# An attention kernel: one of four slices of VectorE's exponentials made in place by an accumulating DMA, with three buffers of clamped scores

## The chip, the cores and the metric

The kernel runs on one core of a Trainium2 chip. A core has five engines that run side by side, each through its own list of instructions in order: PE (TensorE, matrix products), ACT (ScalarE, functions such as exp), DVE (VectorE, elementwise work), POOL (GpSimd, elementwise work and DMA) and SP (SyncE, here only for starting DMAs). They wait for each other through semaphores. Times are microseconds (us) of the device for one execution; lower is better.

## The reference

One input x (2048 tokens, 640 features) goes through two attention branches of 32 heads with 20 features each. Branch A is full softmax attention; branch B lets each token see itself and the seven tokens 2, 4, ... 14 places before it. A gate mixes the two.

```python
def _A_ref(x, wqkv, wo):
    qkv = (x @ wqkv).reshape(B, S, 3, H, Dh).transpose(2, 0, 3, 1, 4)
    q, k, v = qkv[0], qkv[1], qkv[2]
    scores = jnp.einsum("bhqd,bhkd->bhqk", q, k) * Dh ** -0.5
    o = jnp.einsum("bhqk,bhkd->bhqd", softmax(scores), v)
    return o.transpose(0, 2, 1, 3).reshape(B, S, D) @ wo
...
x = A_x
g = sigmoid((x * gate_w).sum(-1, keepdims=True))
return g * _A_ref(x, A_wqkv, A_wo) + (1 - g) * _B_ref(x, B_wqkv, B_wo)
```

## The kernel before

**Tiling of branch A.** The 2048 queries are cut into 4 chunks of 512, the 32 heads into 8 groups of 4, the 2048 keys into 16 blocks of 128. A *group* is one query chunk with four heads; there are 32 (`GROUPS`). A *unit* is one head, one key block and one query chunk: a 128 x 512 square of scores. A group has 64 units, the whole kernel 2048. PE makes a unit's scores with one matmul (`qk`, L1610); a *tile* is two or three such units in one of two score buffers, and ACT turns a tile into exponentials with one instruction (`exp`, L1634, into `ebuf`). PE then multiplies the exponentials with the values and adds them up in `obank` (`pv`, L1679). A column of ones in the values gives the sum of the softmax.

**VectorE's share.** Some units go to DVE instead of ACT. Such a unit *rides* on a tile of two: its scores stand in the third bank of the tile. DVE adds an offset, clamps at zero and writes 16-bit integers (L1624, into `uD`). Read as bfloat16, such an integer is a piecewise linear approximation of an exponential. Four approximations, shifted against each other by a quarter of an octave, make it accurate: the integers plus 0, 32, 64 and 96 (`SHIFTS`), each with its own weight (`WEIGHTS`). Slice 0 is `uD` itself with the plain values `vA`. For slices 1 to 3 DVE writes a shifted copy (`gen_d`, L860, into `eD`), and POOL makes values multiplied by the weights (L852, into `vS`). PE sums all four slices into `obank`. Up to four units of one key block, one for each head, make a *quad*, so a copy is as long as 128 x 2048. There are two buffers `uD`, two `vS` and three `eD`. A buffer `uD` is locked from the quad's opening (`wanted`) until its copies are made and PE's use of slice 0 is in the list; the buffer `uD[1]` also serves as scratch for the gate (`gtr`, `gen_gate`).

**The rest.** Branch B runs alongside, a piece at a time: projections, products on DVE (L945 and L1042, into `NCH` = 3 chunks of the tile `stage`), sums of the products on PE (L955, L1052). At a group's end DVE transposes the sums (`gen_norm`, L821) and POOL scales them (L827, L833). The two branches' output projections run on PE through the helper at L620. The matmuls of L1700 are fillers: PE makes them where it would idle, and nothing uses their result.

**What sets the order.** A planner in the kernel's own Python (`_Sched`, and the loop at the end of `_build`) lays out every engine's list before the kernel runs. It keeps a clock for each engine with a cost for each kind of instruction, and a set of generators (`gen_...`) from which it takes side work when an engine is about to idle. 18 settings of this planner (how long to wait, when a ride is taken, priorities) come from the table `PLAN`, a row for each stretch of tiles. The order within a list is fixed then; on the chip each instruction waits for the semaphores of what it needs. `pv_slot` takes the slices of a quad in order, 0 to 3, and quads one after the other (`cur["pv"]`, `cur["k"]`).

```python
T("dve", 0.065 + 0.1334 * n, lambda e, k=k, sl=sl: e.tensor_scalar(
    eD[:, sl % NS, 0:512 * n].bitcast(I16), uD[d % 2][:, 0:512 * n].bitcast(I16), SHIFTS[k], None, op0=ALU.add),
  reads=[("uD", d % 2, i) for i in range(n)], writes=[("eD", sl % NS)], port=True)
```

These lines record one shifted copy: engine, the planner's cost, the instruction, and the buffers it reads and writes, from which the waits follow.

Of the kernel before, what the change touches and what calls it, by code (L numbers as in the profile page):

```python
# [14 lines left out]
P = 128  # L15
S = 2048
D = 640
# [33 lines left out]
    0: ((0.29, 0.69), 0.16, 1.0, 5.5, 0.94, -1.37, 0.17, 9.99, 7.0, 7.54, 0.6, 0.62, 5.69, 5.04, 0.0, 0.65, 2, -3),  # L51
    5: ((0.29, 0.69), 0.16, 1.0, 6.6, 1.12, -1.6, 0.17, 11.8, 7.0, 7.54, 0.6, 0.62, 4.85, 4.42, 0.0, 0.65, 2, -3),
    10: ((0.32, 0.69), 0.16, 1.0, 6.6, 1.17, -1.6, 0.17, 11.8, 7.0, 7.54, 0.6, 0.62, 4.85, 4.42, 0.0, 0.65, 2, -3),
    15: ((0.34, 0.51), 0.25, 1.0, 5.5, 0.85, -1.26, -0.43, 13.15, 7.0, 7.41, 0.7, 0.51, 8.13, 4.81, 0.12, 0.67, 1, -3),
    25: ((0.3, 0.63), 0.25, 1.0, 2.5, 1.39, -1.06, 0.05, 7.4, 7.0, 8.84, 0.7, 0.51, 4.4, 4.81, 0.08, 0.69, 1, -3),
    30: ((0.3, 0.63), 0.25, 1.0, 2.5, 1.39, -1.06, -0.43, 7.4, 7.0, 8.84, 0.7, 0.51, 4.4, 4.81, -0.2, 0.69, 1, -3),
    35: ((0.32, 0.68), 0.31, 2.5, 5.5, 0.76, -1.58, -0.5, 11.8, 7.0, 6.64, 0.35, 0.39, 4.4, 4.35, 0.26, 0.66, 2, -3),
    40: ((0.29, 0.69), 0.16, 1.0, 5.5, 0.94, -1.37, 0.17, 9.99, 7.0, 7.54, 0.6, 0.62, 5.69, 5.04, 0.0, 0.65, 2, -3),
    45: ((0.26, 0.66), 0.39, 1.0, 2.5, 0.49, -1.34, -0.97, 12.9, 7.0, 8.25, 0.52, 0.47, 4.4, 4.0, 0.0, 0.71, 3, 0.0),
    55: ((0.32, 0.64), 0.35, 1.0, 2.5, 0.49, -1.34, -0.97, 11.8, 7.0, 8.25, 0.64, 0.47, 4.4, 3.34, 0.0, 0.71, 1, 0.0),  # L60
    60: ((0.32, 0.64), 0.35, 1.0, 2.5, 0.49, -1.41, -0.97, 11.8, 7.0, 8.25, 0.64, 0.47, 4.4, 3.34, 0.0, 0.64, 1, 0.0),
    65: ((0.32, 0.64), 0.16, 1.0, 2.5, 0.94, -1.41, -0.97, 11.8, 7.0, 8.25, 0.64, 0.47, 4.4, 3.34, 0.0, 0.54, 2, -3),
    70: ((0.32, 0.64), 0.16, 1.0, 2.5, 0.94, -1.41, -0.97, 11.8, 7.0, 8.25, 0.62, 0.47, 4.4, 4.29, 0.0, 0.54, 2, -3),
    75: ((0.32, 0.64), 0.16, 1.0, 2.5, 0.94, -1.41, -0.97, 11.8, 7.0, 8.62, 0.62, 0.47, 4.4, 4.29, 0.0, 0.54, 2, -3),
    85: ((0.32, 0.64), 0.16, 1.0, 6.6, 0.94, -1.41, -0.97, 11.8, 7.0, 8.62, 0.62, 0.47, 4.4, 4.29, 0.0, 0.54, 2, -3),
    90: ((0.32, 0.64), 0.16, 1.0, 6.6, 1.12, -1.6, 0.4, 11.8, 7.0, 7.54, 0.43, 0.55, 4.4, 4.29, 0.0, 0.7, 2, -3),
    95: ((0.3, 0.63), 0.07, 5.5, 6.3, 0.94, -1.06, 0.05, 7.4, 6.7, 8.96, 0.6, 0.67, 3.3, 5.42, -0.14, 0.61, 1, -1.5),
    100: ((0.3, 0.63), 0.07, 5.5, 6.3, 0.94, -1.06, 0.05, 7.4, 2.0, 8.96, 0.6, 0.67, 3.3, 5.42, -0.14, 0.53, 1, -1.5),
    120: ((0.3, 0.63), 0.07, 5.5, 6.3, 0.94, -1.06, 0.05, 7.4, 2.0, 8.96, 0.66, 0.67, 3.3, 5.42, -0.14, 0.53, 1, -1.5),
    125: ((0.3, 0.63), 0.07, 5.5, 6.3, 0.94, -1.06, 0.05, 7.4, 2.0, 8.96, 0.66, 0.67, 4.79, 5.42, -0.14, 0.53, 1, -1.5),  # L70
    135: ((0.23, 0.63), 0.25, 2.5, 2.5, 0.94, -1.37, 0.49, 7.4, 5.5, 6.11, 0.6, 0.67, 7.13, 5.42, 0.0, 0.61, 1, 0),
    145: ((0.23, 0.7), 0.25, 2.5, 2.5, 0.94, -1.37, 0.49, 7.4, 5.5, 6.11, 0.6, 0.67, 7.13, 5.42, 0.0, 0.61, 1, 0),
    150: ((0.23, 0.7), 0.25, 2.5, 2.5, 0.83, -1.37, 0.49, 7.4, 5.5, 6.11, 0.6, 0.67, 7.13, 5.42, 0.0, 0.61, 1, 0),
    155: ((0.3, 0.63), 0.25, 1.0, 2.5, 0.94, -1.29, 0.26, 6.5, 5.5, 6.11, 0.43, 0.43, 6.57, 4.3, 0.0, 0.68, 1, 0),
    160: ((0.31, 0.76), 0.33, 2.5, 2.5, 0.82, -1.6, -0.34, 11.8, 6.2, 6.64, 0.61, 0.44, 4.4, 4.12, 0.0, 0.48, 2, 0),
    165: ((0.31, 0.7), 0.33, 2.5, 1.0, 0.82, -1.6, -0.34, 11.8, 7.0, 6.64, 0.61, 0.44, 4.4, 4.12, 0.0, 0.63, 2, 0),
    170: ((0.31, 0.7), 0.33, 2.5, 1.0, 0.82, -1.6, -0.34, 11.8, 5.5, 6.64, 0.61, 0.44, 4.4, 4.12, 0.0, 0.63, 2, 0),
    175: ((0.31, 0.7), 0.33, 2.5, 1.0, 0.82, -1.87, -0.34, 9.79, 5.5, 6.64, 0.61, 0.44, 4.4, 4.12, 0.0, 0.63, 2, 0),
    180: ((0.31, 0.7), 0.33, 2.5, 1.0, 0.82, -1.87, -0.35, 9.79, 5.5, 6.64, 0.61, 0.44, 4.4, 4.12, -0.2, 0.63, 2, 1),
    200: ((0.31, 0.76), 0.28, 2.5, 1.0, 0.72, -1.6, -0.5, 9.86, 6.7, 6.64, 0.52, 0.59, 3.16, 3.17, 0.0, 0.78, 2, 0),  # L80
    210: ((0.31, 0.76), 0.28, 2.5, 1.0, 0.72, -1.6, -0.5, 9.86, 6.7, 6.64, 0.52, 0.59, 3.16, 3.17, 0.0, 0.87, 2, 0),
    220: ((0.31, 0.76), 0.28, 2.5, 1.0, 0.72, -1.6, -0.5, 9.86, 6.7, 5.58, 0.52, 0.59, 3.16, 3.66, 0.0, 0.87, 2, -1.5),
    225: ((0.31, 0.76), 0.28, 2.5, 1.0, 0.94, -1.6, -0.5, 9.86, 5.5, 5.58, 0.52, 0.54, 3.16, 3.66, 0.0, 0.87, 2, -1.5),
    235: ((0.31, 0.72), 0.28, 2.5, 1.0, 0.94, -1.6, -0.5, 9.86, 5.5, 4.93, 0.52, 0.54, 4.64, 3.66, 0.0, 0.87, 2, -1.5),
    240: ((0.31, 0.72), 0.28, 2.5, 1.0, 0.94, -1.6, -0.5, 9.86, 7.0, 6.01, 0.45, 0.54, 4.64, 3.66, 0.0, 0.87, 2, -1.5),
    245: ((0.39, 0.72), 0.28, 2.5, 1.0, 0.94, -1.6, -0.5, 9.86, 7.0, 6.01, 0.45, 0.54, 4.64, 3.66, 0.0, 0.87, 0, -1.5),
    250: ((0.39, 0.72), 0.28, 2.5, 1.0, 0.94, -1.6, -0.5, 9.86, 7.0, 6.01, 0.45, 0.54, 6.04, 3.66, 0.0, 0.87, 0, -6),
    255: ((0.39, 0.72), 0.28, 2.5, 1.0, 0.94, -1.6, -0.48, 9.86, 7.0, 6.01, 0.35, 0.54, 6.04, 3.66, 0.0, 0.87, 0, -6),
    260: ((0.29, 0.69), 0.16, 1.0, 1.0, 0.94, -1.37, 0.17, 9.99, 7.0, 7.54, 0.6, 0.62, 5.69, 5.04, 0.0, 0.65, 2, -1.5),
    265: ((0.29, 0.69), 0.16, 1.0, 1.0, 0.94, -1.37, 0.17, 9.99, 7.0, 7.54, 0.6, 0.62, 5.69, 5.04, 0.0, 0.54, 2, -3),  # L90
    270: ((0.3, 0.63), 0.07, 2.5, 2.5, 1.39, -1.06, 0.05, 7.4, 5.5, 8.84, 0.6, 0.67, 4.4, 5.42, 0.0, 0.69, 1, -3),
    275: ((0.23, 0.63), 0.25, 2.5, 2.5, 0.94, -1.29, 0.49, 7.4, 5.5, 6.11, 0.43, 0.43, 5.56, 3.83, 0.0, 0.61, 1, 0),
    290: ((0.23, 0.66), 0.25, 2.5, 2.5, 0.94, -1.29, 0.49, 7.4, 5.5, 6.11, 0.43, 0.43, 5.56, 3.83, 0.0, 0.61, 1, 0),
    300: ((0.23, 0.66), 0.25, 2.5, 2.5, 0.94, -1.05, 0.49, 7.4, 2.0, 5.3, 0.43, 0.43, 5.56, 3.83, 0.0, 0.61, 1, 0),
    310: ((0.23, 0.66), 0.25, 2.5, 2.5, 0.94, -1.05, 0.49, 7.4, 2.0, 5.3, 0.43, 0.43, 5.64, 3.83, 0.0, 0.61, 1, 0),
    320: ((0.3, 0.66), 0.25, 2.5, 2.5, 0.94, -1.05, 0.49, 7.4, 2.0, 5.3, 0.43, 0.43, 5.64, 3.83, 0.0, 0.61, 1, 0),
    330: ((0.3, 0.66), 0.25, 2.5, 2.5, 0.94, -1.05, 0.49, 7.4, 2.0, 5.3, 0.63, 0.43, 5.64, 3.83, 0.0, 0.61, 1, 0),
    340: ((0.3, 0.66), 0.25, 2.5, 2.5, 0.94, -1.05, 0.49, 7.4, 2.0, 5.3, 0.63, 0.52, 5.64, 3.83, 0.0, 0.61, 1, 0),
    345: ((0.3, 0.66), 0.25, 2.5, 2.5, 0.73, -1.17, 0.49, 7.4, 2.0, 5.3, 0.63, 0.52, 5.64, 3.24, 0.0, 0.61, 1, 0),
    365: ((0.3, 0.66), 0.25, 2.5, 2.5, 0.73, -1.17, 0.49, 7.4, 2.0, 5.3, 0.63, 0.52, 5.64, 3.24, 0.0, 0.75, 1, 0),  # L100
    375: ((0.29, 0.69), 0.16, 1.0, 1.0, 0.94, -1.37, 0.17, 9.99, 7.0, 7.54, 0.6, 0.62, 5.69, 5.04, 0.0, 0.65, 2, -3),
    380: ((0.29, 0.69), 0.43, 1.0, 2.5, 0.94, -1.29, 0.17, 7.4, 2.0, 6.11, 0.6, 0.43, 5.56, 5.04, 0.0, 0.65, 2, 0),
    395: ((0.3, 0.63), 0.25, 1.0, 2.5, 0.94, -1.29, 0.26, 6.5, 5.5, 6.11, 0.43, 0.43, 6.57, 4.3, 0.0, 0.68, 1, 0),
    400: ((0.3, 0.63), 0.25, 1.0, 2.5, 0.94, -1.29, 0.26, 6.5, 5.5, 6.11, 0.43, 0.75, 6.57, 4.3, -0.1, 0.43, 1, 0),
    405: ((0.3, 0.63), 0.16, 1.0, 2.5, 0.94, -1.46, 0.26, 6.5, 5.5, 7.16, 0.43, 0.75, 6.57, 4.3, -0.1, 0.43, 1, 0),
    410: ((0.3, 0.63), 0.16, 1.0, 2.5, 0.94, -1.46, -0.29, 6.5, 5.5, 7.16, 0.43, 0.75, 6.57, 4.3, -0.2, 0.43, 1, 0),
    415: ((0.3, 0.63), 0.16, 1.0, 1.0, 0.94, -1.46, -0.29, 6.5, 5.5, 7.16, 0.43, 0.75, 6.57, 3.11, -0.2, 0.43, 1, 0),
# [270 lines left out]
def _build(ctx, nc, A_x, A_wqkv, A_wo, B_wqkv, B_wo, gate_w, out):  # L378
# [38 lines left out]
    rcp = sb([P, 16], FP32, "rcp")  # L417
    gA = [sb([P, 16], FP32, "gA%d" % i) for i in range(2)]

    uD = [sb([P, 4 * 512], BF16, "uD%d" % i) for i in range(2)]  # L420
    gtr = uD[1][:, 0:1024].bitcast(FP32)
    NS = 3
    eD = sb([P, NS, 4 * 512], BF16, "eD")
# [373 lines left out]
    def gen_gate(qc):  # L797
        while qc > 1 and not all(done.get(("norm", POS[qc - 2, q])) for q in range(NQ)):
            yield ("cond",)
        while ulock[1]:  # L800
            yield ("cond",)
# [1073 lines left out]
```

## Time and profile before

| | us |
|---|---|
| median of 3 runs (lowest, highest) | 815.27 (813.67, 817.51) |
| the profiled execution | 818.97 |
| its span, first to last instruction | 816.4 |
| ACT: first exponential starts | 19.34 |
| ACT: last exponentials (two from 802.14, 2.45 long) end | 804.59 |
| granted clock of TensorE, mean | 0.991 of full speed |

The page of the profile also shows the span in 40 equal slices; each digit is the busy share in tenths (9 is 90% or more):

```profile
PE   8999999989989999999898988989899999899987
DVE  7588988579999999989999999898999899988964
ACT  4999999999999999999999999999999999999994
POOL 6014111351112111121112111121101221110110
```

A row of a group of instructions names the line, engine and operation, what it writes and reads with shapes, how many there are; then, after the bar, the time in which the group was busy and the mean length of one in ns; then the engine's idle time just before such instructions, and who ended it. A row of a wait gives the waiting instruction, the one waited for, the total, how often, and the longest.

### The profile page before, as it was taken

The page shows a single profiled execution, that of the slowest core. Times are in us where ns is not written, and L with a number is a line of the kernel's source. Part 1 is how long each engine was busy: PE and PEld are TensorE (multiplying, and loading weights), DVE is VectorE, ACT ScalarE, POOL GpSimd, SP SyncE. Part 2 cuts the span into 40 slices and gives each one's busy share as a digit, 9 for nine tenths or more (in the row PEclk, how much of TensorE's full clock was granted, in tenths as well). Part 3 has the DMA queues.
Part 4 walks back from the last instruction along what each step waited for, and adds up shares of the span by engine and source line. Part 5 has one row for each costly group of instructions (what it writes and reads, how often), then busy time and mean ns, then how long its engine had stood idle before and what let it go on. Part 6 is the DMA issues. An engine that isn't in the chain of part 4 may idle for free.

```text
span 816.4 us, 28733 instructions
## 1 busy us (share of the span) xinstructions
PE 753.3 (92%) x12136; PEld 276.9 (34%) x12138; DVE 718.1 (88%) x1228; ACT 782.7 (96%) x736; POOL 149.6 (18%) x207
## 2 busy tenths in 40 slices
PE   8999999989989999999898988989899999899987
PEld 5332222323333332333333332332243333333324
DVE  7588988579999999989999999898999899988964
ACT  4999999999999999999999999999999999999994
POOL 6014111351112111121112111121101221110110
PEclk9999999999999999999999999999999999999999
DMA  9112212201012231100121000303100130030210
GB/s 313 38 26 47 47 25 43 71 5 29 14 31 52 50 71 27 35 20 6 38 57 38 18 26 19 67 19 77 29 17 14 48 66 14 7 71 28 58 46 35
DMA packets 61458, 35.50 MB, mean 43 GB/s; under 512 B 27220, under 2 KB 60132, under 8 KB 61332
## 3 DMA queue, kind: packets, MB, share of 16 engines
q1 hardware_dynamic: 61044, 33.36, 16.7%
q8 instruction: 96, 1.57, 0.8%
q10 hardware_dynamic: 288, 0.33, 0.1%
q14 instruction: 30, 0.25, 0.1%
HBM read 12.00 MB, written 2.62 MB: 18 GB/s over the span
## 4 chain that ended last, share of the span: by engine, by line
DVE 30%; PE 26%; ACT 25%; issue 12%; SPq 5%; DMA 1%; POOL 0%; POOLq 0%; ACTq 0%; DVEq 0%
ACT ebuf L1634 24%; DVE uD L1624 11%; DVE eD L860 8%; PE score L1610 7%; PE obank L1679 7%; PE side L620 7%; DVE stage L945 3%; SPq L927 3%; PE score L620 2%; SPq L767 2%; DVE stage L1042 2%; DVE qkvB L919 1%; DVE oTt L821 1%; DMA stage<-qkvB 1%; PE score L1325 1%
## 5 line engine op out<-in xcount | busy, mean ns | idle before, releaser
L1634 ACT ACTIVATE ebuf<-score 128x1024 bf16<-128x1024 f32 (+1 forms) x704 | 770.8, 1252 | 13.7 <-PE score L1610 11.9
L1610 PE MATMUL score<-qT,kT 32*128 32x512 bf16 x2048 | 279.4, 386 | 36.0 <-ACT ebuf L1634 20.2
L1624 DVE TENSOR_SCALAR uD<-score 128x512 int16<-128x512 f32 x371 | 244.7, 680 | 24.3 <-PE score L1610 23.6
L860 DVE TENSOR_SCALAR eD<-uD 128x2048 int16<-128x2048 int16 (+1 forms) x279 | 194.8, 719 | 2.3 <-PE obank L1679 1.5
L1679 PE MATMUL obank<-ebuf,vA 128*21 128x512 bf16 x1677 | 156.6, 389 | 4.6 <-ACT ebuf L1634 1.6
L1610 PEld LDWEIGHTS score<-qT,kT 32*128 32x128 bf16 x2048 | 69.6, 91 | 266.0 <-ACT ebuf L1634 178.3
L852 POOL TENSOR_TENSOR vS<-vA,vw 128x252 bf16<-128x252 bf16 x93 | 69.1, 745 | 298.2 <-PE obank L1679 246.6
L620 PE MATMUL side<-xT,kvw 128*32 128x256 bf16 (+2 forms) x2720 | 118.1, 287 | 4.9 <-DVE qkvB L919 2.5
L1679 PE MATMUL obank<-eD,vS 128*21 128x512 bf16 x1113 | 99.2, 384 | 0.0
L620 PEld LDWEIGHTS side<-xT,kvw 128*32 128x32 bf16 (+1 forms) x2720 | 62.0, 96 | 49.9 <-issue 19.6
L1679 PEld LDWEIGHTS obank<-ebuf,vA 128*21 128x21 bf16 x1677 | 36.8, 89 | 87.5 <-issue 56.6
L827 POOL TENSOR_TENSOR rcp<-rcp,gA 128x16 f32<-128x16 f32 x31 | 9.0, 291 | 288.8 <-DVE rcp L825 288.8
L1042 DVE TENSOR_TENSOR stage<-stage,eB 128x2048 bf16<-128x2048 bf16 x40 | 49.7, 1255 | 1.0 <-DMA stage<-qkvB 1.0
L945 DVE TENSOR_TENSOR stage<-qkvB 128x2048 bf16<-128x2048 bf16 x40 | 49.6, 1263 | 0.1
L919 DVE CAST qkvB<-side 128x512 bf16<-128x512 f32 (+1 forms) x72 | 42.0, 592 | 4.3 <-PE side L620 4.1
L1679 PE MATMUL obank<-uD,vA 128*21 128x512 bf16 x371 | 36.9, 388 | 0.0
L1679 PEld LDWEIGHTS obank<-eD,vS 128*21 128x21 bf16 x1113 | 27.7, 92 | 18.8 <-issue 2.6
L833 POOL TENSOR_TENSOR oN<-oTt,rcp 128x512 bf16<-128x512 f32 x31 | 32.6, 1053 | 2.4
L620 PE MATMUL side<-woBp,oB 128*32 128x512 bf16 (+1 forms) x500 | 25.4, 304 | 1.3 <-DVE dst L724 0.5
L821 DVE STREAM_TRANSPOSE oTt<-obank 128x512 f32<-128x512 f32 x32 | 22.7, 708 | 4.5 <-PE obank L1679 4.4
L620 PE MATMUL side<-woA_d,oTd 128*32 128x512 bf16 (+1 forms) x496 | 25.7, 303 | 0.0
L620 PE MATMUL side<-xT,WqP 128*32 128x512 bf16 x320 | 24.3, 385 | 0.6 <-DVE qkvB L657 0.3
(170 smaller groups left out, 519.3 us busy)
## 6 DMA issues: line engine op xcount, KB each, us to landing
stage<-qkvB SPq DMA_DIRECT2D x128, 80.6 KB
WqP<-in_A_wqkv_dram SPq DMA_DIRECT2D x16, 160.0 KB
stage<-in_B_wqkv_dram SPq DMA_DIRECT2D x1, 2400.0 KB
oTd<-oN SPq DMA_DIRECT2D x108, 20.0 KB
qT<-dst SPq DMA_DIRECT2D x104, 20.0 KB
out_dram<-outsb SPq DMA_DIRECT2D x12, 160.0 KB
kvw<-in_A_wqkv_dram SPq DMA_DIRECT2D x2, 800.0 KB
oTd<-in_A_x_dram SPq DMA_DIRECT2D x2, 640.0 KB
```

Of the source, the lines that this page charges most:

```text
L620: ins = e.matmul(o[j:k, :], l(j) if callable(l) else l[:, j:k], r, start=(first and i == 0), stop=(last and i == n - 1), skip_group_check= ...
L821: T("dve", 0.625, lambda e: e.transpose(oTt[:, :], obank[:, :]), reads=["obank"], writes=["oTt"])
L833: T(en, c2, lambda e: e.tensor_tensor(oo, ii, ib, ALU.mult), reads=["rcp", "oTt"], writes=["oN0"])
L852: T("pool", 0.607, lambda e: e.tensor_tensor(vS[:, d % 2, :, :], _ap(vA, (kb * NQ + q) * 4 * DV, [[0, K - 1], [1, 4 * DV]]), _ap(vw, 0, [[ ...
L860: T("dve", 0.065 + 0.1334 * n, lambda e, k=k, sl=sl: e.tensor_scalar(eD[:, sl % NS, 0:512 * n].bitcast(I16), uD[d % 2][:, 0:512 * n].bitca ...
L919: t = TB(dvc(n * TOK), lambda e, o=o, i=i: e.tensor_copy(o, i), reads=[("side", b)], writes=[key])
L945: TB(dvc(CH, 2), lambda e: e.tensor_tensor(o, i0, i1, ALU.mult), reads=["qB", "kB"], writes=[("prod", i)] + (["stage"] if u == 0 else []), ...
L1042: TB(dvc(CH, 2), lambda e: e.tensor_tensor(o, i0, i1, ALU.mult), reads=["eB"] + [("vR", w4) for w4 in range(4)], writes=[("prod", i)], por ...
L1610: ins = e.matmul(o, kT[32 * j:32 * j + 32, q, kb * P:(kb + 1) * P], qT[g % NQT][32 * j:32 * j + 32, :], start=True, stop=True)
L1624: t = T("dve", 0.598, lambda e: e.tensor_scalar(uD[d % 2][:, 512 * i:512 * (i + 1)].bitcast(I16), side[x], UOFF, 0.0, op0=ALU.add, op1=ALU ...
L1634: exps[s] = T("act", actc(512 * n), lambda e: e.activation(ebuf[s % NE][:, 0:512 * n], score[s % 2][:, 0:512 * n], ACTF.Exp, scale=LN2 / S ...
L1679: ins = e.matmul(obank[32 * j:32 * j + DV, :], v, src, start=(kb == 0), stop=(last and k >= len(lst) - 4), skip_group_check=True)
```

## The change

- Slices 1 and 2 are still copies that DVE makes (`eD`). Slice 3 is no copy any more: once PE's use of slice 0 is in the list, POOL starts a DMA that adds 96 to the quad's `uD` in place, reading a row of the constant (`shf`) over and over; it waits for PE's slice 0 and for DVE's two copies. PE then uses `uD` a second time, with the third weight.
- A buffer `uD` stays locked until PE's use of slice 3 is in the list. There are three of them now (`NU` = 3), three `vS`, and two `eD` (`NS` = 2).
- PE takes slices of up to two quads or more in one group, in mixed order: while the DMA of one quad is under way, slices 0 to 2 of the next may come first (`slices_next`, `kq`).
- The gate's transpose has a tile of its own, and gates follow each other; `close` waits until the previous group's scaling is in the list, and early on until the gate is.
- Branch B's products have two chunks instead of three (`NCH`).
- The table `PLAN` has other rows throughout.

```diff
@@ -48,106 +48,101 @@
 PLAN = {
-    0: ((0.29, 0.69), 0.16, 1.0, 5.5, 0.94, -1.37, 0.17, 9.99, 7.0, 7.54, 0.6, 0.62, 5.69, 5.04, 0.0, 0.65, 2, -3),
+    0: ((0.32, 0.64), 0.35, 1.0, 2.5, 0.49, -1.41, -0.97, 11.8, 7.0, 8.25, 0.64, 0.47, 4.4, 3.34, 0.0, 0.64, 1, 0.0),
...
@@ -417,9 +412,10 @@
-    uD = [sb([P, 4 * 512], BF16, "uD%d" % i) for i in range(2)]
-    gtr = uD[1][:, 0:1024].bitcast(FP32)
-    NS = 3
+    NU = 3
+    uD = [sb([P, 4 * 512], BF16, "uD%d" % i) for i in range(NU)]
+    gtr = sb([P, 512], FP32, "gtr")
+    NS = 2
...
+    shf = sb([P, 512], I16, "shf")
...
-    NCH = 3
+    NCH = 2
...
-    vS = sb([P, 2, K - 1, 4 * DV], BF16, "vS")
+    vS = sb([P, NU, K - 1, 4 * DV], BF16, "vS")
...
+        T("dve", 0.2, lambda e: e.memset(shf[:, :], SHIFTS[K - 1]), writes=["shf"])
...
@@ -797,20 +795,18 @@
-        while ulock[1]:
+        while qc and not done.get(("gate", qc - 1)):
             yield ("cond",)
-        ulock[1] = True
...
@@ -847,24 +843,30 @@
-        while cur["pv"] < d - 1 or not done.get(("v", kb, q // 4)) or not done.get("vw"):
+        while cur["pv"] < d - NU + 1 or not done.get(("v", kb, q // 4)) or not done.get("vw"):
             yield ("cond",)
...
-        for k in range(1, K):
+        for k in range(1, K - 1):
...
         done[("dq", d)] = True
         while not done.get(("p0", d)):
             yield ("cond",)
-        ulock[d % 2] = False
+        keys = [("uD", d % NU, i) for i in range(n)]
+        T("pool", 6.0, lambda e: e.dma_start(uD[d % NU][:, 0:512 * n].bitcast(I16), _ap(shf, 0, [[0, n], [1, 512]]), accum_op=ALU.add),
+          reads=["shf"] + keys, writes=keys, dma=True, iss=1.0)
+        done[("ds", d, K - 1)] = True
+        while not done.get(("p3", d)):
+            yield ("cond",)
+        ulock[d % NU] = False
...
@@ -1747,40 +1756,52 @@
+    def slices_next(force, end_g):
+
+        out = []
+        for d in range(cur["pv"], len(dquads)):
+            if dquads[d][0] != pvg or not closed[d]:
+                break
+            while ridden[d] and kq[d] < K and len(out) < K - 1:
+                k = kq[d]
+                if k == K - 1 and not done.get(("p0", d)):
+                    break
+                if not done.get(("ds", d, k)):
+                    if not (force and end_g):
+                        break
+                    urge(d, DHIGH)
+                    run_until(("ds", d, k), DHIGH)
+                elif not end_g and sch.ready(*slice_keys(d, k)) > sch.avail["pe"]:
+                    break
+                out.append((d, k))
+                kq[d] += 1
+            if ridden[d] and kq[d] < K - 1:
+                break
...
+        return out
```

## The prediction

> **What bounds the kernel now.** I read four views, in this order: the page's busy shares, a table of stretches, the instruction groups with shapes kept apart, and the list of who waited for whom.
>
> ```profile
> PE 753.3 (92%) x12136; PEld 276.9 (34%) x12138; DVE 718.1 (88%) x1228; ACT 782.7 (96%) x736; POOL 149.6 (18%) x207
> ```
>
> ScalarE (ACT) is busiest, but PE and VectorE (DVE) are close. A mean can hide a stage with another limit, so next come the stretches: length, then busy time (and count) of PE, weight loads, DVE, ACT, POOL, then clock, DMA share, GB/s.
>
> ```profile
> 10.00:15.00 5.00, 4.88 (x51) 3.17 (x50) 3.90 (x5) 3.20 (x4) 4.55 (x7) 1.00 1.09 345
> ...
> 100.00:200.00 100.00, 92.75 (x1274) 30.50 (x1274) 80.37 (x139) 95.03 (x91) 27.56 (x29) 0.97 0.16 37
> 200.00:300.00 100.00, 94.32 (x1607) 35.82 (x1608) 95.90 (x155) 99.17 (x92) 16.51 (x23) 1.00 0.18 41
> ...
> 600.00:700.00 100.00, 92.68 (x1571) 34.98 (x1568) 92.85 (x152) 99.75 (x93) 16.79 (x23) 1.00 0.14 32
> ```
>
> From 200 us on ACT is busy 99 of every 100 us, with DVE at 93 to 96 behind it. POOL is nearly idle.
>
> ```profile
> L1634 ACT ACTIVATE ebuf<-score 128x1024 bf16<-128x1024 f32 x435 | 424.8, 1082 | 10.0 <-PE score L1610 8.3
> L1634 ACT ACTIVATE ebuf<-score 128x1536 bf16<-128x1536 f32 x269 | 382.6, 1526 | 3.7 <-PE score L1610 3.6
> L1624 DVE TENSOR_SCALAR uD<-score 128x512 int16<-128x512 f32 x371 | 244.7, 680 | 24.3 <-PE score L1610 23.6
> L860 DVE TENSOR_SCALAR eD<-uD 128x2048 int16<-128x2048 int16 x276 | 193.4, 721 | 2.3 <-PE obank L1679 1.5
> L1679 PE MATMUL obank<-eD,vS 128*21 128x512 bf16 x1113 | 99.2, 384 | 0.0
> ```
>
> The 704 exponentials of ACT take 424.8 + 382.6 = 807.4 us by these rows (neighbours overlap a little, so this is above ACT's union), and ACT was idle only 10.0 + 3.7 = 13.7 us ahead of them. So the end moves with the number of 512-column units that ACT must take. A two-unit exponential costs 424.8/435 = 0.977 us, a three-unit one 382.6/269 = 1.422, hence a unit 0.446 us. Units on DVE cost one clamp (L1624, 244.7/371 = 0.66 us) each and three shifted copies (L860, 0.70 us of busy time each) for every four units.
>
> ```profile
> PE score L1610 <- ACT ebuf L1634: 20.2, 52, 1.0
> PEld obank L1679 <- DVE eD L860: 20.1, 75, 0.8
> PEld score L1610 <- DVE uD L1624: 16.8, 29, 1.2
> ACT ebuf L1634 <- PE score L1610: 11.9, 24, 2.0
> PE score L1610 <- DVE uD L1624: 10.9, 26, 0.8
> ```
>
> PE waits for DVE about as much as for ACT (20.1 + 16.8 + 10.9 us against ACT's), but little reaches ACT: 11.9 us.
>
> **The change, part by part,** with counts from the built programs' instruction lists.
>
> *ACT.* Units on DVE go from 371 to 388, so ACT has 1660 instead of 1677. Its exponentials become 459 of two units, 247 of three and one of one. 459 x 0.977 + 247 x 1.422 + 0.53 (0.977 - 0.446) = 800.2 us against 807.4: **-7.2 us** on the engine that sets the end.
>
> *DVE.* Shifted copies fall from 279 to 194: 82 long ones at 0.70 and three short ones at 0.5 are gone, -59 us. 17 more clamps at 0.66 add 11.2. The setting of `shf` (0.3 us, by the 0.27 of the L512 memset) lies in the start, where DVE idles 10 of 30 us. Net -47.5 us, so DVE falls to about 671. On the path this is worth nothing by itself: ACT is full already.
>
> *PE.* Weighted sums rise from 3161 to 3212 matmuls, 51 x 0.089 (99.2/1113) = +4.5 us; the filler matmuls fall from 568 to 484, -7.5 us. They fill idle time, so I count 0 for both. Cover: PE's 6 to 8 idle us in 100; without it +4.5.
>
> *POOL and DMA: the new operation.* Each of 97 quads gets one DMA from POOL's queue that adds 96 to 128 x 2048 16-bit values (0.5 MB) in place. It starts when PE has used the clamped scores and DVE has made both copies, and PE uses its result as the last slice. Nothing like it is in the trace: all DMAs come from SP and ACT, none accumulates. Bounds by the nearest rows (the first three are start, length and issue on SP's queue; the last two are steps of the chain of waits):
>
> ```profile
> 4.28 1.38 SPq L500 DMA_DIRECT2D ebuf<-in_A_wqkv_dram  x1
> 8.38 2.04 SPq L505 DMA_DIRECT2D gwT<-in_gate_w_dram  x1
> 13.22 0.37 SPq L1440 DMA_DIRECT2D stage<-in_B_wqkv_dram  x1
> ...
> 332.40 1.69 DMA qT<-qbnd
> 658.63 2.94 DMA stage<-qkvB
> ```
>
> Issue 0.37 to 2.04 us; landing of a small DMA 1.69 to 2.94; moving 0.52 MB at the 345 GB/s of the 10 to 15 us row is 1.5 us once, and up to 4.5 if source, destination and result follow each other. Together 3.6 to 9.5 us; I take 6.5, the middle, for no row is nearer to one end.
>
> What is available? In the new lists I counted the exponentials between the later of the two releases and the matmul group of PE that waits for the DMA, each at 0.977 or 1.422 + 0.02 us. Over 97 quads this is 7.4 us at the least, 9.8 in the median, 14.1 at most. At 6.5 us none is late: **0 us**. At 9.5, 47 are late by 45 us in total, or 6 us if one exponential in stock (1.1 us) covers each; at 3.6, 0. Queued behind a waiting DMA on POOL are the next quad's weighted values (L852, 0.745 us) and the scaling of a finished group (L833); PE needs the former with that quad's second slice, the latter only for the output projection. POOL's own load, 150 us, has room for 97 x 2.04 = 198 more. SP's small DMAs share the 16 engines with 51 MB more; the wait for them that is on the page is small (DVE 1.0 us).
>
> *Buffers.* Two product buffers instead of three in branch B (L945, L1042): those products wait 1.1 us now; if each of 80 waited for the sums that free its buffer (15.2 us of L955 over 40 = 0.38 us) it would be 30 us of DVE, inside the 47.5 freed: 0. The same cover holds for two `eD` buffers instead of three. The gate's transpose gets a tile of its own: a lock less, 0.
>
> *The order.* The table of planner settings is replaced, so nearly every instruction moves. Bounds: ACT's 13.7 us of idle time could vanish, or every stretch could be like 100 to 200 us (5 of 100 idle): 38 of 760 us, less the 9.4 idle between 30 and 789 us now, +28. I take 0, by the later stretches, which all have the same limit. At the end, the last sum of branch B now stands behind the last score, and the work that before began 1.4 us ahead of the last exponential's end (803.15 against 804.6) follows it: **+1 us**, of 0 to 1.4.
>
> Sum: -7.2 + 1 = **-6.2 us**. The profiled execution took 818.97 us (span 816.4 and 2.6 around it), 3.7 above the median of 815.27. Carried over, 812.8 for such an execution and **809.0 as median**.
>
> **Rivals.**
>
> (1) *The slice lands late (slower).* PE runs in order, so a group that waits for the DMA holds the next scores and ACT behind it. It decides from 7.4 us of landing time. At 10 us, 59 are late by 71 us raw, 20 after the stock of one exponential: 815.3 - 6.2 + 20 = 829. At 11 us, 65 after stock: 874. For it: my upper bound is 9.5, and one mechanism could stretch the issue: POOL and DVE get in each other's way. The same copy on DVE takes:
>
> ```profile
> L860 DVE TENSOR_SCALAR eD<-uD x279: 550/683/1840, 43.7 to 786.8; 128x2048 int16<-128x2048 int16 x138, 128x1536 int16<-128x1536 int16 x2
> ```
>
> Median 683 ns, at most 1840. If POOL can't work during such copies and the products (194 x 0.70 + 80 x 1.26 = 237 of 760 us, 31%), an issue of 2.04 becomes 3.0, and the upper bound 10.5 us. Against: at 6.5 it becomes about 7.0, still in time. The Trainium skill (SBUF — State Buffer, "Who interferes with whom") states such a lock: a DMA issued from GpSimd starves for descriptors while VectorE holds the shared port in a two-port mode. The 1840 ns agree that something holds; no run here shows a DMA held.
>
> (2) *DVE pays back (no change to slower).* The reverse: each DMA's issue on POOL stops a copy. Once by 1840 - 683 = 1.16 us is 97 x 1.16 = 112 us, which exceeds 47.5 by 65; in the 500 us from 200 to 700 that is 43 on top of some 470, 13 more than fit: 828. It decides from 47.5/97 = 0.49 us a DMA. Against: only few copies are so long now (the mean is 38 ns above the median) with 207 instructions on POOL.
>
> (3) *ACT stays less full (within 0.5%).* The new order and the contention for DMA engines leave 6 us more of idle time: 815. For: more tiles of two units, which give PE less time for each; against: DVE's relief shortens the 47.8 us in which PE waited for it.
>
> (4) *More than forecast.* The idle 13.7 us shrink by half as DVE no longer holds score banks: 809 - 7 = 802.
>
> That the change doesn't do what it says is excluded: the lists show 97 DMAs and 85 copies fewer.
>
> **Chances.** Forecast 0.47, (4) 0.13, (3) 0.17, (1) 0.14, (2) 0.09. A measurement here can tell about 0.5% (4.1 us) from no change. Faster: 0.60; same 0.17; slower 0.23. The forecast's own range is 804 to 811; the range that takes in the others is 800 to 826, which leaves out some 0.05 below and 0.12 above (most of (1), half of (2)).
>
> **What would show it.** Right: exponentials of ACT sum to about 800 us with no more than 14 us idle before them; DVE near 671; no row in which PE waits for the DMA; copies still near 0.70 us. Wrong: PE's groups at the weighted sum waiting for that DMA, landing above 7.4 us (rival 1); copies well above 0.72 us (2); ACT idle above 20 us before exponentials with PE waiting for something else (3).

## The result, and the profile after

| | before | after |
|---|---|---|
| median of 4 runs (lowest, highest), us | 816.31 (813.67, 817.51) | 898.17 (894.59, 901.12) |
| span of the profiled execution, us | 816.4 | 899.3 |
| clock granted to TensorE, mean | 0.991 | 0.945 |

The changed kernel is slower: its time is 1.100 of the time before (95% interval 1.095 to 1.105). The forecast was 809 us and its range ended at 826.

The page of the changed kernel: busy time of each engine; then the POOL DMA queue's packets, MB and share of 16 engines; then the new DMA's size and its median time from issue to landing.

```profile
PE 777.3 (86%) x12103; PEld 279.3 (31%) x12105; DVE 696.6 (77%) x1161; ACT 781.4 (87%) x739; POOL 282.5 (31%) x308
...
q0 software_dynamic: 51216, 50.86, 39.1%
...
uD<-shf POOLq DMA_DIRECT2D x97, 512.0 KB, 6.3
```

No engine is full any more. ACT works as long as before (781.4 us against 782.7) in a span that is 83 us longer. DVE has less to do, as intended. The packets of the new queue take 39.1% of the time of all 16 DMA engines, 3.62 us for each of the 97 DMAs (0.391 x 899.3 / 97). (Packets can overlap on an engine, as shares above 1 below show, so this is packet time, at most the time for which a DMA holds the engines.) Where ACT stood idle is in the groups with shapes kept apart (after the second bar: idle time ahead of the group, and who ended it):

```profile
L1638 ACT ACTIVATE ebuf<-score 128x1024 bf16<-128x1024 f32 x459 | 444.8, 1057 | 77.8 <-PE score L1614 75.9
L1638 ACT ACTIVATE ebuf<-score 128x1536 bf16<-128x1536 f32 x247 | 348.0, 1499 | 17.6 <-PE score L1614 16.9
```

Before, 13.7 us of idle time lay ahead of the exponentials; now it is 77.8 + 17.6 = 95.4. The difference, 81.7, is nearly the whole 82.9 us by which the span grew. ACT waits for scores, so PE is late. The list of waits says what for (total, times, longest):

```profile
ACT ebuf L1638 <- PE score L1614: 92.8, 71, 8.9
PEld obank L1684 <- DMA uD<-shf: 24.1, 26, 2.4
PE obank L1684 <- DMA uD<-shf: 16.6, 21, 1.9
DVE stage L1044 <- DMA stage<-qkvB: 16.5, 4, 9.0
```

Two causes show. The first is the DMA that makes slice 3: the weighted sums wait for it, each time for 2.4 us at most. Its two rows must not be added. PEld is the weight load ahead of a matmul, and both rows mostly hold the same wait:

```profile
418.37 0.10 PEld L1684 LDWEIGHTS obank<-ebuf,vA 128*21 128x21 bf16 x4 [0.65 <-DMA uD<-shf]
418.37 0.40 PE L1684 MATMUL obank<-ebuf,vA 128*21 128x512 bf16 x4 [0.35 <-DMA uD<-shf]
```

Of the 21 waits of PE, 19 overlap one of a weight load; taken together they cover 25.3 us, of which the matmuls stood still for 16.6. ACT's longest waits are 8.9 us, which no such wait explains. They resemble the last row: DVE waits four times for `stage<-qkvB`, SP's shifted copies of branch B's values, up to 9.0 us. In the trace of before this wait was 1.0 us in total:

```profile
DVE stage L1042 <- DMA stage<-qkvB: 1.0, 2, 0.5
```

One of the four, in time order (start, length, engine, instruction; in brackets the idle time before it and who ended it):

```profile
423.93 2.41 DVE L1044 TENSOR_TENSOR stage<-stage,eB 128x2048 bf16<-128x2048 bf16 x2 [8.96 <-DMA stage<-qkvB]
426.26 0.68 DVE L921 CAST qkvB<-side 128x512 bf16<-128x512 f32 x1
426.99 0.62 PE L1054 MATMUL side<-stage,Rep 128*32 128x256 bf16 x8 [8.01 <-DVE qkvB L921]
428.34 1.02 ACT L1638 ACTIVATE ebuf<-score 128x1024 bf16<-128x1024 f32 x1 [8.94 <-PE score L1614]
```

SP's loads land late; DVE, in order, holds the products (L1044) and behind them the emptying of a `side` bank (L921); PE, in order, waits for that, and no scores come; ACT stands for 8.94 us. Each engine's list passes the same 9 us on. What the DMA engines did meanwhile is in the table of stretches (columns as in the prediction):

```profile
413.00:416.00 3.00, 2.79 (x53) 1.19 (x50) 1.40 (x2) 3.00 (x3) 1.71 (x3) 1.00 1.14 182
...
420.00:422.00 2.00, 0.00 (x0) 0.00 (x0) 0.00 (x0) 0.00 (x0) 0.00 (x0) 1.00 1.09 183
422.00:424.00 2.00, 0.00 (x0) 0.00 (x0) 0.07 (x1) 0.00 (x0) 0.04 (x1) 0.61 0.27 64
```

The DMA share (last column but one) is above 1 until 422 us: all 16 engines are full while every compute engine stands still. It falls to 0.27 in the next 2 us, and DVE goes on at 423.93. Three slice DMAs had been issued at 407.75, 410.59 and 414.44 us.

The hole costs more than its length. The granted clock (last column but two) is 1.00 while PE stands still at first, 0.61 from 422 to 424, and 0.50 from 424 to 432; so PE, back at work at 426.99, made matmuls of 512 columns in 0.61 us instead of 0.39. Over the whole execution the clock was 0.945.

### The profile page after: what moved, and what is told of

It reads as the page before. It is cut to its first block, busy times and chain, and to the rows that moved or that the text cites. A ratio compares the mean times of both kernels' runs of the same rounds, so it can differ in the third digit from the quotient of the medians.

```text
span 899.3 us, 28906 instructions
## 1 busy us (share of the span) xinstructions
PE 777.3 (86%) x12103; PEld 279.3 (31%) x12105; DVE 696.6 (77%) x1161; ACT 781.4 (87%) x739; POOL 282.5 (31%) x308
## 3 DMA queue, kind: packets, MB, share of 16 engines
q0 software_dynamic: 51216, 50.86, 39.1%
## 5 line engine op out<-in xcount | busy, mean ns | idle before, releaser
L1638 ACT ACTIVATE ebuf<-score 128x1024 bf16<-128x1024 f32 (+1 forms) x707 | 769.4, 1210 | 95.4 <-PE score L1614 92.8
L1614 PE MATMUL score<-qT,kT 32*128 32x512 bf16 x2048 | 288.0, 398 | 37.8 <-ACT ebuf L1638 22.7
L1628 DVE TENSOR_SCALAR uD<-score 128x512 int16<-128x512 f32 x388 | 257.7, 680 | 64.8 <-PE score L1614 64.1
L864 POOL DMA_DIRECT2D uD<-shf x97 | 130.3, 1344 | 202.9 <-DVE eD L856 118.6
L1684 PE MATMUL obank<-ebuf,vA 128*21 128x512 bf16 x1660 | 162.0, 400 | 23.0 <-DMA uD<-shf 15.3
L856 DVE TENSOR_SCALAR eD<-uD 128x2048 int16<-128x2048 int16 x194 | 145.3, 764 | 8.4 <-PE obank L1684 7.5
L618 PE MATMUL side<-xT,kvw 128*32 128x256 bf16 (+2 forms) x2720 | 122.8, 296 | 9.3 <-DVE qkvB L921 7.0
L848 POOL TENSOR_TENSOR vS<-vA,vw 128x252 bf16<-128x252 bf16 x97 | 103.0, 1080 | 82.0 <-PE obank L1684 54.0
L618 PEld LDWEIGHTS side<-xT,kvw 128*32 128x32 bf16 (+1 forms) x2720 | 65.6, 98 | 54.6 <-issue 20.9
L1684 PE MATMUL obank<-eD,vS 128*21 128x512 bf16 x776 | 69.0, 388 | 0.8 <-POOL vS L848 0.8
L1044 DVE TENSOR_TENSOR stage<-stage,eB 128x2048 bf16<-128x2048 bf16 x40 | 51.3, 1302 | 16.5 <-DMA stage<-qkvB 16.5
L921 DVE CAST qkvB<-side 128x512 bf16<-128x512 f32 (+1 forms) x72 | 42.0, 593 | 21.8 <-PE side L618 12.2
L1684 PE MATMUL obank<-uD,vS 128*21 128x512 bf16 x388 | 39.9, 402 | 1.5 <-DMA uD<-shf 1.4
```

The costliest lines, as they stand in the source:

```text
L618: ins = e.matmul(o[j:k, :], l(j) if callable(l) else l[:, j:k], r, start=(first and i == 0), stop=(last and i == n - 1), skip_group_check= ...
L848: T("pool", 0.607, lambda e: e.tensor_tensor(vS[:, d % NU, :, :], _ap(vA, (kb * NQ + q) * 4 * DV, [[0, K - 1], [1, 4 * DV]]), _ap(vw, 0, [ ...
L864: T("pool", 6.0, lambda e: e.dma_start(uD[d % NU][:, 0:512 * n].bitcast(I16), _ap(shf, 0, [[0, n], [1, 512]]), accum_op=ALU.add), reads=[" ...
L921: t = TB(dvc(n * TOK), lambda e, o=o, i=i: e.tensor_copy(o, i), reads=[("side", b)], writes=[key])
L1044: TB(dvc(CH, 2), lambda e: e.tensor_tensor(o, i0, i1, ALU.mult), reads=["eB"] + [("vR", w4) for w4 in range(4)], writes=[("prod", i)], por ...
L1614: ins = e.matmul(o, kT[32 * j:32 * j + 32, q, kb * P:(kb + 1) * P], qT[g % NQT][32 * j:32 * j + 32, :], start=True, stop=True)
```

## The experiments

Theory A: the slice's DMA costs twice, by landing late for PE, and by filling the 16 engines so that SP's small DMAs land late. Theory B: the new order and the tables of the planner are worse by themselves. Other rivals are named in the expectations. These number their theories each in its own way: in those of e1_tiny, e2_aside, e4_pool and e5_dve, theory 1 is the filled engines and theory 2 the late slice (the two halves of A here), and theory 3 is the order (B here); the A and B of the others are explained there. Ratios are to the kernel before, with 95% intervals. A difference between two of these kernels carries some 2 to 5 us by these intervals. All kernels but one keep the changed kernel's order of instructions on every engine. The diffs are cut to the part of each line that changes.

**No DMA at all.** The slice's DMA is not issued and nobody waits for it; PE sums the clamped scores a second time where slice 3 should be.

```diff
+                        if t.dom == "dma" and sname == "pool":
+                            continue
...
+                            if d.dom == "dma" and d.stream == "pool":
+                                continue
```

> The DMA of each quad is dropped from POOL's list with all waits for it; every other list stays in the order of the changed kernel. It leaves out the shift in slice 3. What is left is the new order alone, with DVE's and ACT's work as forecast. Theory A (the order is worth the 6 us of the sum, and in the run with the small transfer POOL's 97 issues of 0.9 us and the holding of DVE ate them): 806 to 811 us, ACT's idle time ahead of its exponentials back to about 14 us from 22.5. Theory B (the order itself keeps ACT less full): like the run with the small transfer, 815 to 820 us.

Measured: 817.17 us (12 runs), ratio 1.0021 (1.0002 to 1.0040). The order alone gives no gain (theory B of this expectation), and the DMA costs the whole 81 us from there to 898. ACT's groups, and an early stretch of e8_none and then of the kernel before:

```profile
L1643 ACT ACTIVATE ebuf<-score 128x1024 bf16<-128x1024 f32 x459 | 444.8, 1095 | 13.7 <-PE score L1619 12.6
L1643 ACT ACTIVATE ebuf<-score 128x1536 bf16<-128x1536 f32 x247 | 349.6, 1532 | 6.2 <-PE score L1619 5.6
...
30.00:100.00 70.00, 66.94 (x982) 22.28 (x977) 60.20 (x107) 65.18 (x64) 15.91 (x18) 1.00 0.16 35
```

```profile
30.00:100.00 70.00, 67.67 (x972) 21.81 (x965) 57.46 (x109) 69.43 (x65) 13.61 (x15) 1.00 0.17 35
```

ACT's busy time fell by 8.0 us (774.7 against 782.7), as the change promises. But it is idle 19.9 us ahead of the exponentials instead of 13.7, and 9.27 us behind the last instead of 7.18. -8.0 + 6.2 + 2.1 = +0.3: the span is 816.6 against 816.4. Most of the added idle time is early: from 30 to 100 us ACT is busy 65.18 us, in the kernel before 69.43.

**A tiny DMA.** Everything stays (issue, waits, the place in POOL's list), but the DMA adds to 32 columns only.

```diff
-uD[d % NU][:, 0:512 * n].bitcast(I16), _ap(shf, 0, [[0, n], [1, 512]]), accum_op=ALU.add
+uD[d % NU][:, 0:32].bitcast(I16), shf[:, 0:32], accum_op=ALU.add
```

> The accumulating DMA of each quad moves only the first 32 of its up to 2048 columns; every list of instructions, every wait and POOL's issues stay as in the changed kernel. It leaves out the shift of the other columns in slice 3. Theory 1 (the transfers fill the 16 DMA engines, and small DMAs of SP that branch B needs land late behind them) and theory 2 (the slice itself lands later than PE's wait for it): both lose their cause, so the time falls from 898 to what the new order is worth, 807 to 820 us, PE's waits for the quad's DMA fall from 41 us to under 5 and DVE's and POOL's waits for the branch B DMA from 37 to about the 14 us of before. Theory 3 (the new order, or POOL's issues that hold DVE and POOL up, cost the time): stays above 870 us.

Measured: 819.39 us (10 runs), ratio 1.0053 (1.0025 to 1.0081); landing 2.3 us in the median, 5.0 at most. No wait of PE for this DMA shows. So issuing 97 DMAs on POOL (0.90 us each here) costs 2.2 us in all, hardly clear of the noise. The size makes the rest.

**Half the bytes, and the same bytes without the addition.** First, the left 256 of each 512 columns only; second, a plain copy that overwrites the scores with the constant.

```diff
-uD[d % NU][:, 0:512 * n].bitcast(I16), _ap(shf, 0, [[0, n], [1, 512]]), accum_op=ALU.add
+_ap(uD[d % NU], 0, [[512, n], [1, 256]]).bitcast(I16), _ap(shf, 0, [[0, n], [1, 256]]), accum_op=ALU.add
...
+uD[d % NU][:, 0:512 * n].bitcast(I16), _ap(shf, 0, [[0, n], [1, 512]])
```

> Each DMA adds to the first 256 of every 512 columns only: half the bytes, the same number of rows, all lists and waits the same. It leaves out the shift of the other half in slice 3. If the loss is in proportion to the engines' time (39% of the span for full, 2.8% for the small transfer: 819 to 898 us): about 855 to 860 if bytes count, 890 if rows count. If it comes from bursts that fill the engines (three transfers in 7 us need more than 7 us only at the full size): nearer to the small transfer, 822 to 840.

> The same DMA as a plain copy: it overwrites the quad's clamped scores with the constant instead of adding to them, so slice 3 is left out in effect; size, packets, releases, waits and lists stay. If reading the destination is what fills the engines (three passes, 3.6 us of all 16 engines for each DMA), the queue's share falls from 39% to about 26 or less, landing from 6.3 to 4.5 to 5.2 us, and the time to 835 to 860. If the 512 rows of 1 KB set the price whatever is done with them: share and time as in the changed kernel, 885 to 900.

Measured: half 842.8 us, ratio 1.0335 (1.0307 to 1.0362); plain 837.85, ratio 1.0270 (1.0248 to 1.0291). The queue's row of the plain copy:

```profile
q0 software_dynamic: 13968, 50.86, 18.4%
```

The plain copy's time lies in the first range of its expectation; its packets, which that text took to stay, did not. The same 50.86 MB take 13968 packets instead of 51216, and 18.4% of 16 engines instead of 39.1%: 1.59 us a DMA (330 GB/s) against 3.62 (145 GB/s). Bytes are not the measure, then; the time for which a DMA fills the engines is. In the order of that time (0.24 us tiny, 1.59 plain, 2.34 half, 3.62 whole) the loss over e8_none is 2.2, 20.7, 25.6 and 81.0 us. The half DMA misses all the ranges of its expectation; it is nearest to that of the bursts, 3 us above it. It also settles a rival: it has the same 51216 packets as the whole DMA and the same work on POOL (1.35 us an issue), and yet loses 25.6 us instead of 81.0, so POOL's issuing is not what costs the rest.

**Traffic without waiting.** The same accumulating DMA goes to a spare array in HBM, and PE and DVE don't wait for it (the first four write it plainly). Slice 3 is not made.

```diff
+                            if d.dom == "dma" and d.stream == "pool" and sname != "pool":
+                                continue
...
+    aside = nc.dram_tensor("aside", [4, P, 2048], I16)
...
-e.dma_start(uD[d % NU][:, 0:512 * n].bitcast(I16), _ap(shf, 0, [[0, n], [1, 512]]), accum_op=ALU.add)
+e.dma_start(aside[d % 4, :, 0:512 * n], _ap(shf, 0, [[0, n], [1, 512]]), **({"accum_op": ALU.add} if d > 3 else {}))
```

> The same DMA with the same size, releases and place in POOL's list, but it accumulates into a spare array in HBM, and neither PE nor DVE waits for it; all lists in the same order. It leaves out the shift in slice 3 (slice 3 uses the clamped scores as they are). The transfers stay and the lateness of the slice is gone. Theory 1 (engines filled, SP's small DMAs late): most of the loss stays, 860 to 890 us, with ACT's long gaps behind branch B. Theory 2 (late slice): falls to 815 to 835 us.

Measured: 860.86 us, ratio 1.0529 (1.0492 to 1.0566), with nearly the same load on the DMA engines (3.52 us of packet time a DMA). The two rows of it that matter:

```profile
ACT ebuf L1641 <- PE score L1617: 56.6, 47, 7.6
...
DVE stage L1047 <- DMA stage<-qkvB: 17.8, 3, 7.6
```

So traffic for which nobody waits costs 43.7 us (860.9 - 817.2), and the step from here to the changed kernel, in which slice 3 is waited for, is 37.3 (898.2 - 860.9). The waits for slice 3 make a part of this step directly. Between the two profiled executions the span differs by 40.8 us: PE, with the same 12103 matmuls, was idle 23.5 us longer, 16.6 of them in waits for slice 3, and busy 17.3 us longer (777.3 against 760.0), at a mean granted clock of 0.945 against 0.970. That the waits brought the clock down is likely from the hole above, but no run shows it. DVE's wait for SP's loads is as long as with the whole change. The target in HBM is a difference that this pair of kernels can't remove.

**Which traffic?** Of those 97 DMAs, 30 are left out: first those around SP's eight batches of loads `stage<-qkvB`, then, as a control, 30 far from them.

```diff
+LEFT = [17, 18, 19, 20, 21, 22, 26, 27, 28, 39, 40, 41, 42, 49, 50, 51, 58, 59, 60, 61, 71, 72, 73, 84, 85, 86, 87, 91, 92, 93]
...
+                        if t.left:
+                            continue
```

> As e2_aside (the slice's transfer goes to a spare array in HBM, nobody waits for it, slice 3 isn't added), but 30 of the 97 transfers are left out: those that in the trace of e2_aside were issued from 8 us before SP's loads of branch B's chunks (stage<-qkvB, eight batches) to 3 us after them. e2_aside was 43.7 us above e8_none, which has no transfers at all. Theory A (the traffic costs time because SP's loads for branch B land late behind it): most of the loss goes, 820 to 835 us (1.005 to 1.023 of the kernel before), and the wait of VectorE for stage<-qkvB falls from 17.8 us to under 6. Theory B (traffic costs time wherever it is, in proportion to it): 67/97 of the loss is left, 817 + 30 = 847 us, the wait for stage unchanged in its share.

> The control to e11_clear: again 30 of the 97 transfers are left out, but only such as lie more than 25 us ahead of a batch of those loads or 12 us behind it. Theory A: the loss stays nearly whole, 850 to 861 us (1.041 to 1.053), wait for stage<-qkvB 14 to 20 us. Theory B: 847 us, as e11_clear.

Measured: 832.52 us, ratio 1.0202 (1.0158 to 1.0246), without the DMAs around the loads; 855.37, ratio 1.0471 (1.0431 to 1.0511), without others. The same 31% less traffic gives back 28.3 us in one place and 5.5 in the other. The wait of ACT for scores in e11_clear:

```profile
ACT ebuf L1653 <- PE score L1629: 32.7, 40, 3.4
```

and in e12_other, with that of DVE for the loads:

```profile
ACT ebuf L1653 <- PE score L1629: 54.1, 47, 8.1
...
DVE stage L1059 <- DMA stage<-qkvB: 15.9, 3, 8.2
```

The 8 us holes are gone in the first (DVE's wait for `stage<-qkvB` is 2.5 us there) and whole in the second. Both results lie in theory A's ranges. Of the 43.7 us, 28.3 go with the DMAs that meet these loads, 22.8 more than with as many elsewhere; the 5.5 of the control is hardly clear of the noise. The other 15.4, left with 67 DMAs elsewhere, were not taken further apart.

**The constant from HBM.** The source's rows become 4 KB long instead of 1 KB: the constant is kept in an array `far` in HBM.

```diff
-uD[d % NU][:, 0:512 * n].bitcast(I16), _ap(shf, 0, [[0, n], [1, 512]]), accum_op=ALU.add
+uD[d % NU][:, 0:512 * n].bitcast(I16), far[:, 0:512 * n], accum_op=ALU.add
```

> The accumulating DMA reads its constant from an array in HBM with 4 KB rows, so that source and destination are 128 rows of 4 KB instead of 512 of 1 KB; the same bytes, lists and waits, and the full result. If the number of packets sets the engines' time: the queue's share falls from 39% to under 20, landing under 5 us, time 825 to 850. If the bytes set it (0.5 MB at 145 GB/s): share and time about as in the changed kernel, 880 to 905.

Measured: 866.51 us, ratio 1.0629 (1.0604 to 1.0654), neither theory's number. Packets fall to the plain copy's 13968, yet a DMA still takes 2.98 us of the engines (plain 1.59) and lands in 5.5 in the median. So the number of packets is not all of it: of the 2.03 us between plain and accumulating DMA this saves 0.64. The loss over e8_none, 49.3 us, falls into the order of engine time above (2.98 lies between 2.34 and 3.62). The rest may be the addition or the read from HBM; these runs don't part the two.

**Slice 3 by POOL, without a DMA.**

```diff
-e.dma_start(uD[d % NU][:, 0:512 * n].bitcast(I16), _ap(shf, 0, [[0, n], [1, 512]]), accum_op=ALU.add)
+e.tensor_scalar(uD[d % NU][:, 0:512 * n].bitcast(I16), uD[d % NU][:, 0:512 * n].bitcast(I16), SHIFTS[K - 1], None, op0=ALU.add)
...
+    for t in flip:
+        t.dom = "cmp"
```

> POOL adds the 96 itself, in place, with one instruction on the 16-bit integers at the place in its list where it issued the DMA; the lists of all engines stay in the same order and the result is the full one. No DMA traffic, so theory 1 expects SP's small DMAs as quick as before. POOL's instruction is estimated at 2.1 to 4.3 us for 2048 elements (from 1.05 us for 512 of the output scaling and 1.04 us for 1024 pairs of the constant copy), 200 to 420 us in all beside 153: if DVE is not held, 807 to 825 us; if each holds a copy of DVE for half its length, 97 x 1 to 2 us come back on DVE and the time is 830 to 870. Theory 3 (order): above 870.

Measured: 1138.46 us, ratio 1.3942 (1.3907 to 1.3977). This was a miss: one addition takes POOL 5.36 us, not 2.1 to 4.3, and it holds DVE's copies, of which the row gives lowest, median and highest length:

```profile
L857 DVE TENSOR_SCALAR eD<-uD x194: 618/694/5875, 46.0 to 1110.1; 128x2048 int16<-128x2048 int16 x194
```

A copy that starts during an addition ends only after it (beside the addition from 302.13 to 307.99 us, a copy ran from 304.65 to 308.54); the longest took 5875 ns. So this kernel says nothing on the order or the waits; it shows that the DMA is not the worst way.

**Slice 3 by DVE, in place.**

```diff
-        T("pool", 6.0, lambda e: e.dma_start(uD[d % NU][:, 0:512 * n].bitcast(I16), _ap(shf, 0, [[0, n], [1, 512]]), accum_op=ALU.add),
-          reads=["shf"] + keys, writes=keys, dma=True, iss=1.0)
+        yield ("dve", DAHEAD, sch.free(*keys))
+        T("dve", 0.065 + 0.1334 * n, lambda e: e.tensor_scalar(uD[d % NU][:, 0:512 * n].bitcast(I16), uD[d % NU][:, 0:512 * n].bitcast(I16), SHIFTS[K - 1], None, op0=ALU.add),
+          reads=keys, writes=keys, port=True)
```

> DVE makes slice 3 in place (97 more instructions of 0.7 us, 68 us more on DVE, some 765 in all); three buffers and the mixed order of slices stay, planner settings as in the changed kernel, so the order around it moves. All theories that blame the DMA (1, 2): no DMA, near the kernel before, 812 to 835 us, since DVE carries what it carried before and the settings do not fit. Theory 3 (mixed order and three buffers are bad): above 850.

Measured: 972.57 us, ratio 1.1921 (1.1881 to 1.1960). Inconclusive: with the work on DVE the planner laid out another order (376 units on DVE instead of 388, and ACT waiting 107 us for branch B). Its result is also wrong, from a cause that was not found. Its time is not used. One of its rows is a caution: without any slice DMA, DVE waits 26.3 us for `stage<-qkvB` there, so an order can bring this wait too; the comparisons above hold the order fixed.

No kernel tried is faster than the one before. The kernel before with the same traffic beside it was not run.

## Why the prediction was wrong, step by step

*The bound: right as an account.* ACT's idle time ahead of the exponentials explains 81.7 of the 82.9 us. But ACT, busy 87% of the span, no longer sets the end; PE's late scores do.

*ACT, -7.2 us: right.* Counts are as predicted, 459, 247 and one. The rows give 444.8 + 348.0 + 0.6 = 793.4 us where 800.2 stood; with the same overlap of neighbours in both, ACT's busy time in e8_none is 8.0 us lower. In the changed kernel itself it is only 1.3 lower; an exponential that starts after a wait overlaps no neighbour, which may be why.

*DVE, about 671 us: mis-sized, without effect.* It is 696.6. Without the DMA it is 683.7, so 12.9 us come with the DMA; copies took 764 ns against 729 without it (194 x 0.035 = 6.8 us of that). DVE is at 77% of the span.

*The new DMA, 0 us: this step failed, by 37.3 us.* The landing time was nearly right: 6.5 us were taken, 6.3 is the median. That was partly luck, for 6.5 was the middle of 3.6 to 9.5. But the step compared one number with the slack of all 97 DMAs. The view of the tile `shf` gives lowest, median and highest:

```profile
DMA to landing us min/median/max: 5.4/6.3/9.8
```

DMAs come in bursts, three in 7 us, and one takes the engines 3.62 us. Of the 97, 21 took more than the 7.4 us of the least slack, and 19 of these were issued within 4.4 us of the one before. The counted slack also ran from the release of the DMA, while POOL issues it only when the work ahead in its list is done. What the runs showed instead of 0 is the 37.3 us; 25.3 us of waits are a part of it. The fit in the Trainium skill (DMA: Bandwidth & Descriptors, "Anatomy of one DMA — SWDGE (gpsimd) path"), 2.0 us and 436 GB/s, gives an estimate of 3.2 us for this size; the plain copy measured 3.9 in the median, the accumulating one 6.3.

*"SP's small DMAs share the 16 engines with 51 MB more; the wait for them that is on the page is small": this step failed worst.* It put at nothing a traffic that costs 43.7 us with nobody waiting for it, 28.3 of them with the DMAs that meet these loads. The wait of 1.0 us was measured with the engines busy for 14 to 18% in the long stretches; it says nothing of what the wait will be when they are full. SP's queue shows it; the same batch of 16 loads in e8_none, then in the changed kernel (start, time for all issues):

```profile
375.39 11.33 SPq L934 DMA_DIRECT2D stage<-qkvB  x16
```

```profile
402.36 16.17 SPq L929 DMA_DIRECT2D stage<-qkvB  x16
```

The issues alone stretch by 4.8 us, and DVE gets the last bytes 5.4 us behind the last issue (418.5 to 423.9), in e8_none 1.5 us (386.7 to 388.3). The other batches show it less or more: seven of the eight took 10.5 to 12.0 us in e8_none and 13.0 to 18.1 in the changed kernel (the first took 18.5 and 19.0). The Trainium skill says that DMAs started by different engines run on the same 16 DMA engines and interleave, and that a second issuing engine saves only the time of issuing (DMA: Bandwidth & Descriptors, "Issuing engines are not separate DMA queues"); this trace agrees, with 16.17 us beside POOL's DMAs against 11.33 without them.

*Order 0, tail +1: mis-sized.* Together they were +8.3 us (6.2 of idle time and 2.1 at the end), and used up ACT's gain. The bounds (-13.7 to +28) held it; "by the later stretches" was the wrong choice, for the loss is in the early ones too.

*Buffers 0, POOL's load: right as far as seen.* Two buffers of products cost nothing that a wait shows; POOL's issue took 1.27 to 1.97 us, inside the bounds. POOL's weighted values (L848) took 1.08 us each instead of the 0.745 that was taken; PE's matmuls waited 3.5 us for them.

*The rivals.* (1), the late slice, was right in its mechanism: waiting for the slice makes 37 of the 81 us. Its working let late DMAs come from a longer landing of all, not from bursts. (2) came true in its sign only, 35 ns a copy. (3) named the contention for DMA engines, with 6 us for it and the order together; it was 43.7 and 8.3. The 47.8 us of PE's waits for DVE in it add waits of matmuls to those of their weight loads; without counting the same time twice they are 42.6. Both causes of the loss were thus named, and both priced from a trace in which the DMA engines were mostly idle.

## What to carry to other kernels

A DMA that takes work off an engine is to be costed as work of the 16 DMA engines: engine time for each (here 3.62 us for 0.5 MB), how many come in a burst, and which other transfers fall into it. Ask of each such transfer what stands behind its waiting instruction on an engine that runs in order, for that decides whether 9 us of delay cost nothing or cost 9 us on four engines. Compare the slack with the latest landing in a burst, not with the median.

## What the runs showed of the hardware

- Accumulating into SBUF from a row of 1 KB read over and over took 3.62 us of all 16 engines for 512 KB, the plain copy 1.59; 528 packets a DMA against 144.
- POOL's time to issue such a DMA was 0.80 us for the plain copy, 0.90 for the tiny one and with the HBM source, 1.34 for the one with 528 packets.
- An addition of 128 x 2048 16-bit integers took POOL 5.36 us, DVE about 0.69; DVE copies that met it lasted up to 5.88.
- POOL's weighted values (128 x 252, bf16) took 1.08 us beside accumulating DMAs of 528 packets, 0.70 beside plain copies of 144, 0.72 without a DMA.
- TensorE's granted clock fell with its idle time: 0.991 before, 0.945 after, 0.50 from 424 to 432 us, from within the hole at 420 until PE had worked for 5 us again. The same 12103 matmuls kept PE busy for 777.3 us there, 752.5 in e8_none (clock 0.987).
